# An attention loop in periods of two steps: one whole and two half visits of values, and one pair of score blocks reduced through a relu of key differences

## The chip, the cores and the metric

The kernel runs on one core of a Trainium2 chip. The core has five engines that run beside each other and meet through semaphores: TensorE (PE, with its weight loads shown as PEld), VectorE (DVE), ScalarE (ACT), GpSimd (POOL) and SyncE (SP, which issues the DMAs here). The metric is the device time of one execution in microseconds (us); the text gives the median of several runs.

## What is computed

One transformer block on x of 2048 rows by 448 columns, in float32: a layer norm, attention with 16 query heads of 28 columns that share one key and one value head, a residual add, a second layer norm, a gated feed-forward part of 1792 columns, and a second residual add.

```python
q = (x @ wq).reshape(B, S, H, Dh).transpose(0, 2, 1, 3)     # x here: the normed x
k = x @ wk
v = x @ wv
scores = jnp.einsum("bhqd,bkd->bhqk", q, k) * (Dh ** -0.5)
p = softmax(scores)
o = jnp.einsum("bhqk,bkd->bhqd", p, v)
h = x_in + o.transpose(0, 2, 1, 3).reshape(B, S, H * Dh) @ wo
h2 = h + (silu(n(h) @ w1) * (n(h) @ w3)) @ w2               # n: layer norm
```

## The kernel before

**Numbers.** Most operands are kept as a rounded high part and a low part (fp32r); a product is then three matmuls: high by high, high by low, low by high. For the scores, `KH` and `KL` are the keys' parts, and `QS[i]` holds the queries' (`qh`, `ql`). Values and exponentials are plain float32, whose matmul the chip runs as two passes: each appears twice in the profile.

**Units of work.** Four heads lie in the four strips of 32 rows (`lane(j)`), so four score matmuls with 32 rows each can run side by side. A *unit* i of the attention is one block of 512 queries by four heads; there are 16. A unit has 16 *chunks* of 128 keys, and a *step* s is one chunk of one unit: 256 steps in all.

**What a step does.** For each of the four heads, three matmuls put the transposed scores of 128 keys by 512 queries into a PSUM bank (`Head.mm`, line 293; parts a, b and c of the order below), ACT takes the exponential (`Head.exp`, line 302) into a tile `pt`, and `pv` (line 310) multiplies it with the values `VA[:, c]` into the accumulator `po`. In `pv` the four heads stand side by side in strips of 32 columns, and not of rows. A visit of `pv` takes either all 512 queries of a chunk or a half of them.

**The maxima.** The exponentials need each query's maximum score. It is found 20 steps ahead (`AHEAD`): in each step four *units of the maximum* (class `Unit`, named u0 to u3 after the head) multiply 128 queries by 512 keys (line 241) into a bank, and DVE reduces it (line 246). When a unit i is through, `max_done` (lines 270 to 275) takes the maximum over the four key blocks on DVE, moves it on POOL and transposes it on DVE, and `max_out` (line 281) sends it by four DMAs into a spare row (28 of each strip) of the queries, against which the keys have a row of ones: so the score matmul subtracts the maximum itself. The first 20 steps' maxima are found in the start by `quad` (lines 251 to 268), in another way: since max(a, b) = max(b - a, 0) + a, a matmul with the difference of two key blocks (`KD`) goes through a relu on ACT (line 263), and DVE adds the scores of the first block and takes the maximum in one instruction (line 266), one for two blocks.

**The order of the work** is written out by hand. Every engine takes its instructions in the order in which the code emits them. `ORDER` (line 34) is the order of one step: `3a` is part a of head 3, `u2` the maximum of head 2 (matmul and reduction), `w` and `v` are visits of the values. In each step `w` takes the second half of the chunk of two steps ago, and `v` the first half of the last one (`values`, lines 589 to 598). The last 20 steps have no maxima; they follow `LAST_ORDER`, with whole visits. After the visit `v` and at the end of a step, `run` issues what `todo` holds for this step: splits of the next queries (`build_qs`, line 218), the copy and normalisation of an output (lines 314 to 334), output projections (`wo_rows`, lines 341 to 351, with statistics after it), layer norms and their transposes, and loads of weights.

**Banks and buffers.** Seven PSUM banks go round through a list (`bank`, `done`); the eighth is `po`. In SBUF, `qs_pool` has three buffers of 8 KB per partition for the queries (of which half is used) and later for the feed-forward weights (`split_w`), and `p_pool` four buffers of 4 KB, each for the exponentials of two heads, later for the hidden columns.

**Start and end.** The start (to about 95 us) loads, norms and transposes x, and makes keys, values, queries and the first maxima. After the loop comes the feed-forward part, where PE is busy throughout.

Of the kernel before, what the change touches and what calls it, by code (L numbers as in the profile page):

```python
# [16 lines left out]
P = 128  # L17
S = 2048
D = 448
# [14 lines left out]
ORDER = "3a u2 w 0a 2a u1 3b 1a 0b 2b 3c 1b 0c 2c u3 v u0 1c".split()  # L34
# [4 lines left out]
def block_kernel(  # L39
# [25 lines left out]
    qs_pool = ctx.enter_context(tc.tile_pool(name="qs", bufs=3))  # L65
# [9 lines left out]
    pexp = keep.tile([P, NQ], F32, name="pexp")  # L75
    KH = keep.tile([P, S], F32R, name="KH", tag="kh")
# [139 lines left out]
    def build_qs(i, ps=None):  # L216
        t, g = divmod(i, NG)
        QS[i] = qs_pool.tile([P, 4, T], F32R, name="qs")
        qh, ql = QS[i][:, 0], QS[i][:, 1]
        q = QR[t][:, g] if ps is None else ps  # L220
        se.activation(qh, q, AF.Copy)  # L221
        (ge if ps is None else ve).tensor_tensor(ql, q, f(qh), op=ALU.subtract)  # L222
# [7 lines left out]
    class Unit:  # L230
# [5 lines left out]
        def mm(self):  # L236
            i, n, kt, r = self.i, self.n, self.kt, lane(self.j)
            if i not in MX:
                MX[i] = wk_pool.tile([P, 16, 4], F32, name="mx")
            self.ps = bank("pa")  # L240
            pe.matmul(self.ps, QS[i][r, 0, n * P : (n + 1) * P], KH[r, kt * T : (kt + 1) * T],  # L241
                      start=True, stop=True)

        def red(self):
            c = 4 * self.j + self.n
            ve.tensor_reduce(MX[self.i][:, c, self.kt : self.kt + 1], self.ps, axis=AX.X, op=ALU.max)  # L246
            done(self.ps)
# [3 lines left out]
    def quad(i, n, kp, diff):  # L251
        for j in range(4):
            if i not in MX:
                MX[i] = wk_pool.tile([P, 16, 4], F32, name="mx")
                ge.memset(MX[i], LOW)
            ps = RL[j, diff] = bank("pa")
            ks = KD[:, kp] if diff else KH[:, 2 * kp * T : (2 * kp + 1) * T]
            pe.matmul(ps, QS[i][lane(j), 0, n * P : (n + 1) * P], ks[lane(j)], start=True, stop=True)
        for j in range(4):
            ps = RL.pop((j, diff))  # L260
            if diff:
                r = RL[j] = (wk_pool if j % 2 else sp).tile([P, T], F32, name="rb", bufs=2)
                se.activation(r, ps, AF.Relu)
            else:
                r = RL.pop(j)
                ve.tensor_tensor_reduce(r, ps, r, 1.0, LOW, op0=ALU.add, op1=ALU.max,
                                        accum_out=MX[i][:, 4 * j + n, 2 * kp : 2 * kp + 1])
            done(ps)
# [8 lines left out]
    def max_out(i):  # L277

        dst = f(QS[i][28::32, 0]).rearrange("j (n b x) -> j n b x", n=NQ, b=4)
        for b in range(4):  # L280
            sy.dma_start(dst[:, :, b], NGT[i % 2][32 * b : 32 * b + 16])

    class Head:
# [14 lines left out]
        def exp(self):  # L298
            i, c, (p, jj) = self.i, self.c, divmod(self.j, 2)
            if (i, c, p) not in PT:  # L300
                PT[i, c, p] = p_pool.tile([P, 2, T], F32R, name="pt")
            se.activation(f(PT[i, c, p][:, jj]), self.ps, AF.Exp, bias=0.0, scale=SCALE)  # L302
            done(self.ps)

    def pv(i, c, h0, h1):
# [3 lines left out]
        for j in range(4):  # L309
            pe.matmul(PO[i][32 * j : 32 * j + 32, q], VA[:, c], f(PT[i, c, j // 2][:, j % 2, q]),  # L310
# [71 lines left out]
    with tc.tile_pool(name="start", bufs=1) as sp:  # L382
        wq_r = wo_r = OT[:, :, :D]
        WQ = [w.rearrange("p c (h r) -> p c h r", h=H) for w in OS]
        wkv_r = sp.tile([P, 4, 96], F32, name="wkv_r")
        WKV = [sp.tile([P, 4, 96], F32R, name=f"WKV{k}") for k in range(2)]
        KD = sp.tile([P, 2, T], F32R, name="KD")
        ones = NGT[1][:64]
        ve.memset(wkv_r, 0.0)
        ve.memset(ones, 1.0)  # L390
        ve.memset(VA, 1.0)
        ve.memset(f(NEG[0]), 0.0)
        for k in range(2):
            ve.memset(f(WQ[k][:, :, :, DH:]), 0.0)
        for m0, w in ((0, wk), (64, wv)):
            load_w(wkv_r[:, :, m0 : m0 + DH], w)
        sy.dma_start(X[1], xv[1])
        load_w(wq_r, wq)
        for t in range(2, NT):
            sy.dma_start(X[t], xv[t])  # L400

        def split_wkv():
            ve.tensor_copy(wkv_r[:, :, 32 : 32 + DH], wkv_r[:, :, :DH])
            se.activation(WKV[0], wkv_r, AF.Copy)
            ge.tensor_tensor(WKV[1], wkv_r, f(WKV[0]), op=ALU.subtract)

        wq4 = wq_r.rearrange("p c (h r) -> p c h r", h=H)

        def low_wq(c0, c1, eng):
            for c in range(c0, c1 + 1):  # L410
                eng.tensor_tensor(WQ[1][:, c, :, :DH], wq4[:, c], f(WQ[0][:, c, :, :DH]), op=ALU.subtract)

        def split_wq(c0, c1, eng=None):
            for c in range(c0, c1 + 1):
                se.activation(WQ[0][:, c, :, :DH], wq4[:, c], AF.Copy)
                if eng:
                    low_wq(c, c, eng)

        def load_wo():
            ge.memset(wo_r, 0.0)  # L420
            wov = wo.rearrange("(g j r) e -> j r g e", j=4, r=DH)
            for j in range(4):
                sy.dma_start(wo_r[32 * j : 32 * j + DH], wov[j])

        def split_wo(g):
            ve.tensor_copy(WO[0][:, g], wo_r[:, g])
            ge.tensor_tensor(WO[1][:, g], wo_r[:, g], f(WO[0][:, g]), op=ALU.subtract)

        def stats(t, *ns):
            for n in ns:  # L430
                ln_stats(t, n)
            if NQ - 1 in ns:
                ln_rstd(t)

        def norm(t):
            for n in range(NQ):
                ln_norm(t, n)

        def tr(t, *cs):
            for c in cs or range(4):  # L440
                ln_tr(t, c)

        def kv(t, between=None):
            cols = slice(t * T, (t + 1) * T)
            ps = bank()
            mm_D(ps[:96], WKV, XT[t], slice(0, 96), slice(0, T), between)
            se.activation(KH[0:64, cols], ps[0:64], AF.Copy)
            ve.tensor_tensor(KL[0:64, cols], ps[0:64], f(KH[0:64, cols]), op=ALU.subtract)
            vt = sp.tile([P, T], F32, name="vt", bufs=2)
            se.activation(vt[64:96], ps[64:96], AF.Copy)  # L450
            sy.dma_start(f(KH[64:128, cols]), f(KH[0:64, cols]))
            sy.dma_start(f(KH[28::32, cols]).rearrange("j (b e) -> j b e", b=16), ones)
            sy.dma_start(f(KL[64:128, cols]), f(KL[0:64, cols]))
            if t % 2:
                ge.tensor_tensor(KD[:, t // 2], f(KH[:, cols]), f(KH[:, (t - 1) * T : t * T]), op=ALU.subtract)
            done(ps)
            return vt

        def va(t, vt):
            ps = bank()  # L460
            for n in range(NQ):
                pe.transpose(ps[:, 32 * n : 32 * n + 32], vt[64:96, n * P : (n + 1) * P], ident[64:96, 64:96])
            ve.tensor_copy(VA[:, NQ * t : NQ * t + NQ, :DH],
                           ps[:, :P].rearrange("p (n r) -> p n r", n=NQ)[:, :, :DH])
            done(ps)

        def q(t, g, between=None):
            ps = bank()
            mm_D(ps, [w[:, :, 4 * g : 4 * g + 4].rearrange("p c h r -> p c (h r)") for w in WQ],
                 XT[t], slice(0, P), slice(0, T), between)  # L470
            if t == g == 0:
                build_qs(0, ps)
            else:
                se.activation(QR[t][:, g], ps, AF.Copy)
            done(ps)

        first = [(quad, i, n, 0, diff) for i, n in ((0, 0), (0, 1), (0, 2), (0, 3), (1, 0)) for diff in (True, False)]
        first += [(quad, 0, n, 1, diff) for n in range(NQ) for diff in (True, False)]
        first += [(max_done, 0), (max_out, 0)]
        first += [(quad, 1, 0, 1, diff) for diff in (True, False)]  # L480

        def quads(n=1):
            while n > 0 and first:
                fn, *args = first.pop(0)
                fn(*args)
                n -= fn is quad

        for n in range(NQ):
            ln_stats(0, n)
            ln_rstd(0, n, n + 1)  # L490
            if n > 0:
                ln_norm(0, n - 1)
# [265 lines left out]
```

## Time and profile before

| what | value |
|---|---|
| median of 3 runs | 1238.77 us (1237.6 to 1239.81) |
| the profiled execution | 1238.6 us, span of its instructions 1236.8 us |
| mean granted TensorE clock | 0.998 |
| busy: PE, PEld, DVE, ACT, POOL | 1209.7, 723.4, 869.2, 677.9, 335.6 us |
| visits of the values, instructions of L310 | 3936 matmuls of 400 ns (eight a visit) |
| exponentials, L302 | 1024 of 604 ns |
| maxima, L246 | 944 of 682 ns |
| score matmuls, L293 (KH, KL) | 2048 of 451 ns, 1024 of 420 ns |

A row of the page's groups reads: line, engine, operation, output<-inputs by the names of the code, shape, number of instructions, then busy time in us and the mean duration of one in ns, then the idle time of that engine just before them, and what ended most of it. Matmuls on different strips overlap, so their summed durations are far more than the busy time. In the page's second part the span is cut into 40 slices, and each digit is the busy share in tenths. In a timeline, a row has its start and its length in us; consecutive instructions of one kind are merged into one row (x4), and the bracket tells how long the engine stood idle before it and what ended that. In the windows view a row has the stretch and its length, then for PE, PEld, DVE, ACT and POOL the busy time with the number of instructions, then the granted clock, the DMA share and the GB/s.

### The profile page before, as it was taken

Reading aid. Unit: us, or ns where it says so; the run is one execution under the profiler, and the core shown is the slowest. Engines: PE = TensorE matmul, PEld = TensorE weight load, DVE = VectorE, ACT = ScalarE, POOL = GpSimd, SP = SyncE. Lnnn points to the kernel's source line nnn. Section 1 sums busy time; section 2 is a strip of 40 time slices with the busy share of each in tenths; the row PEclk is TensorE's granted clock in tenths of the full one; section 3 lists DMA queues with packets and bytes.
Section 4 is the critical chain, followed back from the end, with each engine's and each line's share of the span. In section 5 each row is a group of like instructions: output and inputs, shape, how many; then the busy total and the mean of one; then the engine's idle time right before and its main releaser. Section 6 shows DMA issues by size and latency. Waiting matters only on the chain. (4 is left out here: it accounts for less than half of the span.)

```text
span 1236.8 us, 25401 instructions
## 1 busy us (share of the span) xinstructions
PE 1209.7 (98%) x10492; PEld 723.4 (58%) x10492; DVE 869.2 (70%) x1473; ACT 677.9 (55%) x1291; POOL 335.6 (27%) x266
## 2 busy tenths in 40 slices
PE   6999999999999999999999999999999999999998
PEld 4664444444444444444444443488888888888886
DVE  7759999998899998889998893145444445444333
ACT  3657888886688886688786688721111111121111
POOL 3201101110111110121110110454555555555552
PEclk9999999999999999999999999999999999999999
DMA  5010101000010000010000010013000000000000
GB/s 170 10 36 1 34 3 45 11 11 2 11 28 19 11 12 2 11 36 11 11 11 2 10 45 10 26 57 113 1 8 23 2 1 30 1 1 30 1 1 30
DMA packets 32651, 27.03 MB, mean 22 GB/s; under 512 B 11096, under 2 KB 29208, under 8 KB 32536
## 3 DMA queue, kind: packets, MB, share of 16 engines
q1 hardware_dynamic: 32536, 25.41, 7.1%
q8 instruction: 82, 1.34, 0.5%
q14 instruction: 33, 0.27, 0.1%
HBM read 20.25 MB, written 3.80 MB: 19 GB/s over the span
## 5 line engine op out<-in xcount | busy, mean ns | idle before, releaser
L302 ACT ACTIVATE pt<-pb 128x512 f32<-128x512 f32 x1024 | 530.7, 604 | 144.5 <-PE pb L293 121.4
L246 DVE TENSOR_REDUCE mx<-pa 128x1 f32<-128x512 f32 x944 | 585.7, 682 | 16.6 <-PE pa L241 6.9
L293 PE MATMUL pb<-qs,KH 32*128 32x512 f32 x2048 | 368.1, 451 | 3.2 <-ACT pt L302 0.3
L241 PE MATMUL pa<-KH,qs 32*128 32x512 f32 x944 | 346.2, 467 | 4.0 <-DVE mx L246 1.6
L310 PE MATMUL po<-pt,VA 128*32 128x256 f32 (+1 forms) x3936 | 326.8, 400 | 0.5 <-ACT OT L314 0.5
L293 PE MATMUL pb<-qs,KL 32*128 32x512 f32 x1024 | 275.0, 420 | 0.0
L293 PEld LDWEIGHTS pb<-qs,KH 32*128 32x128 f32 x2048 | 166.6, 182 | 140.4 <-ACT pt L302 89.6
L135 PE MATMUL pa<-xh,qs 128*128 128x512 f32 x784 | 205.6, 395 | 0.0
L241 PEld LDWEIGHTS pa<-KH,qs 32*128 32x128 f32 x944 | 140.6, 181 | 101.7 <-DVE mx L246 93.8
L650 ACT ACTIVATE rb<-pa 128x512 f32<-128x512 f32 x56 | 30.4, 596 | 252.6 <-PE pa L642 252.6
L135 PEld LDWEIGHTS pa<-xh,qs 128*128 128x128 f32 x784 | 146.9, 188 | 33.7 <-issue 1.2
L310 PEld LDWEIGHTS po<-pt,VA 128*32 128x32 f32 x3936 | 79.8, 108 | 135.4 <-issue 126.2
L667 PE MATMUL pb<-w2s,pt 128*128 128x448 f32 x672 | 144.5, 370 | 0.8 <-POOL w2s L365 0.8
L667 PEld LDWEIGHTS pb<-w2s,pt 128*128 128x128 f32 x672 | 123.9, 188 | 20.9 <-issue 10.1
L293 PEld LDWEIGHTS pb<-qs,KL 32*128 32x128 f32 x1024 | 116.0, 183 | 0.9
L357 POOL TENSOR_TENSOR qs<-QR,qs 128x1024 fp32r<-128x1024 f32 x32 | 88.1, 2768 | 98.5 <-DVE qs L356 98.5
L659 DVE TENSOR_TENSOR pt<-rb,pt 128x512 fp32r<-128x512 f32 x56 | 82.4, 1471 | 39.2 <-ACT pt L658 39.2
L356 DVE CAST qs<-QR 128x1024 fp32r<-128x1024 f32 x32 | 21.0, 688 | 120.1 <-PE pa L642 96.3
L135 PE MATMUL pa<-xl,qs 128*128 128x512 f32 x336 | 96.3, 395 | 0.0
L658 ACT ACTIVATE pt<-rb 128x512 fp32r<-128x512 f32 x56 | 35.4, 633 | 81.4 <-DVE rb L655 81.4
L222 POOL TENSOR_TENSOR qs<-QR,qs 128x512 fp32r<-128x512 f32 x15 | 19.3, 1285 | 203.2 <-ACT qs L221 187.1
L135 PEld LDWEIGHTS pa<-xl,qs 128*128 128x128 f32 x336 | 63.3, 189 | 14.8
(100 smaller groups left out, 821.1 us busy)
## 6 DMA issues: line engine op xcount, KB each, us to landing
rb<-sd SPq DMA_DIRECT2D x64, 64.0 KB
QR<-in_B_w_dram SPq DMA_DIRECT2D x16, 192.0 KB
X<-in_A_x_dram SPq DMA_DIRECT2D x3, 896.0 KB
out_dram<-X SPq DMA_DIRECT2D x3, 896.0 KB
w<-in_B_w_dram SPq DMA_DIRECT2D x8, 192.0 KB
w_wo<-in_B_w_dram SPq DMA_DIRECT2D x6, 224.0 KB
qs<-ngt SPq DMA_DIRECT2D x64, 2.0 KB
sm<-OT SPq DMA_DIRECT2D x64, 2.0 KB
```

The lines of the kernel that those rows point to most:

```text
L135: pe.matmul(ps, lhs[b][:, cb, lsl], rhs[a][:, ca, rsl], start=(k == 0), stop=(k == len(terms) - 1 and not part),)
L241: pe.matmul(self.ps, QS[i][r, 0, n * P : (n + 1) * P], KH[r, kt * T : (kt + 1) * T], start=True, stop=True)
L246: ve.tensor_reduce(MX[self.i][:, c, self.kt : self.kt + 1], self.ps, axis=AX.X, op=ALU.max)
L293: pe.matmul(self.ps, (KH, KH, KL)[k][r, c * P : (c + 1) * P], QS[i][r, (0, 1, 0)[k]], start=(k == 0), stop=(k == 2))
L302: se.activation(f(PT[i, c, p][:, jj]), self.ps, AF.Exp, bias=0.0, scale=SCALE)
L310: pe.matmul(PO[i][32 * j : 32 * j + 32, q], VA[:, c], f(PT[i, c, j // 2][:, j % 2, q]), start=(c == 0 and h0 == 0), stop=(c == NC - 1 and ...
L356: ve.tensor_copy(wh, W13[k])
L357: ge.tensor_tensor(wl, W13[k], f(wh), op=ALU.subtract)
L650: se.activation(sg, ps[0], AF.Silu)
L658: se.activation(h[:, 0], sg, AF.Copy)
L659: ve.tensor_tensor(h[:, 1], sg, f(h[:, 0]), op=ALU.subtract)
L667: pe.matmul(Y[t][n][:, :D], hid[a][:, n * P : (n + 1) * P], w2s[:, b, :D], start=(k == 0 and m == 0), stop=(k == NF - 1 and m == 2))
```

## The change

1. The loop with maxima goes by *periods of two steps* s and s+1, with one hand-written order for both. Heads 0 to 3 are those of step s, 4 to 7 those of step s+1; `4c'` and `5c'` are the last parts of the previous period's heads.
2. The values of a period take three visits in place of four: `p0` is a whole visit (step s-2), `p1` and `p2` the two halves of step s-1.
3. Of the eight maxima of a period, two become one pair by the difference of keys, as in the start: `d2` is the matmul with `KD` and a relu on ACT, `t2` the matmul with the first of the two key blocks and DVE's add-and-max. The other six stay as they are.
4. `KD` and the relu's buffer stay for the whole loop. The columns of the maxima become two fixed tiles that are set to a very low value once, at the beginning; the column of the second block of a pair keeps it.
5. In SBUF, ten slots of 4 KB per partition take the place of the pools `qs`, `pt` and `start`: three for the queries, five for the exponentials, one each for `KD` and the relu; in the start and in the feed-forward part the same slots hold other tiles. Each exponential takes the next free half of a slot.
6. What `todo` holds for steps s and s+1 is issued at the end of the period; what stands at half steps comes after `p0`. The transposes of the second layer norm move by one step, to whole periods.

```diff
-ORDER = "3a u2 w 0a 2a u1 3b 1a 0b 2b 3c 1b 0c 2c u3 v u0 1c".split()
+ORDER = ("4c' 5c' u3 p0 d2 0a u1 3a 3b 2a 0b 0c u1 2b 3c p1 "
+         "7a u0 1a 2c 1b 6a 7b 1c u0 6b 7c p2 5a 4a u3 6c 4b 5b t2").split()
...
-    qs_pool = ctx.enter_context(tc.tile_pool(name="qs", bufs=3))
...
+    MXS = [keep.tile([P, 16, 4], F32, name=f"mx{k}") for k in range(2)]
+    slots = ctx.enter_context(tc.tile_pool(name="slots", bufs=1))
+
+    def slot(k, dt, name):
+        return slots.tile([P, 2, T], dt, name=name, tag=f"slot{k}")
+
+    QSP, PTP, WSP, HIDP = [4, 0, 1], [9, 5, 6, 7, 8], [(0, 1), (2, 3), (4, 5)], [6, 7, 8, 9]
+    KD = slot(2, F32R, "kd")
+    RELU = slot(3, F32, "relu")
+
+    def take(ring):
+        ring.append(ring.pop(0))
+        return ring[-1]
...
-        QS[i] = qs_pool.tile([P, 4, T], F32R, name="qs")
+        QS[i] = slot(QSP[i % 3], F32R, "qs")
+        MX[i] = MXS[i % 2]
...
-        def mm(self):
+        def mm(self, diff=False):
...
-            pe.matmul(self.ps, QS[i][r, 0, n * P : (n + 1) * P], KH[r, kt * T : (kt + 1) * T],
-                      start=True, stop=True)
+            ks = KD[:, kt // 2] if diff else KH[:, kt * T : (kt + 1) * T]
+            pe.matmul(self.ps, QS[i][r, 0, n * P : (n + 1) * P], ks[r], start=True, stop=True)
...
+        def relu(self, r):
+            se.activation(r, self.ps, AF.Relu)
+            done(self.ps)
+
+        def both(self, r):
+            ve.tensor_tensor_reduce(r, self.ps, r, 1.0, LOW, op0=ALU.add, op1=ALU.max, accum_out=self.col())
+            done(self.ps)
...
-            i, c, (p, jj) = self.i, self.c, divmod(self.j, 2)
-            if (i, c, p) not in PT:
-                PT[i, c, p] = p_pool.tile([P, 2, T], F32R, name="pt")
-            se.activation(f(PT[i, c, p][:, jj]), self.ps, AF.Exp, bias=0.0, scale=SCALE)
+            if not pair:
+                tl = slot(take(PTP), F32, "pt")
+                pair.extend((tl[:, 0], tl[:, 1]))
+            pt = PT[self.i, self.c, self.j] = pair.pop(0)
+            se.activation(pt, self.ps, AF.Exp, bias=0.0, scale=SCALE)
...
-        ws = qs_pool.tile([P, 4, T], F32R, name="qs")
-        wh, wl = [ws[:, 2 * b : 2 * b + 2].rearrange("p a (c m e) -> p (a c) m e", c=2, m=2) for b in range(2)]
+        wh, wl = [slot(x, F32R, "w").rearrange("p a (c m e) -> p (a c) m e", c=2, m=2) for x in take(WSP)]
...
-            at(e + 33.5 + 2 * c, lambda t, c: ln_tr(t, c, True, True), t, c)
+            at(e + 34.5 + 2 * c, lambda t, c: ln_tr(t, c, True, True), t, c)
...
+    for s in range(0, LAST - AHEAD, 2):
+        us = [u for k in range(2) for u in a_units(s + k + AHEAD)]
+        for op in ORDER:
+            x = int(op[1]) if op[0].isalpha() else 0
+            if op[0] == "p":
+                if s > 0:
+                    pv(*divmod(s - 2 + (x > 0), NC), max(x, 1) - 1, x or 2)
+                if x == 0:
+                    run(s + 0.5)
+            elif op[0] == "d":
+                us[x].mm(True)
+                us[x].relu(RELU[:, s // 2 % 2])
+            elif op[0] == "t":
+                us[x].mm()
+                us[x].both(RELU[:, s // 2 % 2])
+            elif op[0] == "u":
+                u = us[x] if us[x] else us[4 + x]
+                us[x] = None
+                u.mm()
+                u.red()
+            else:
+                h = int(op[0])
+                head(s + h // 4 - 2 * (op[-1] == "'"), h % 4, "abc".index(op[1]))
+        run(s)
+        run(s + 1)
...
-            h = p_pool.tile([P, 2, T], F32R, name="pt")
+            h = slot(take(HIDP), F32R, "hid")
```

The rest of the diff indents the start anew and follows from these lines.

More of the change, by code (lines that the diff above doesn't have):

```diff
@@ L251, in quad @@
     def quad(i, n, kp, diff):
[L252 to L268, printed above, removed]
+        us = [Unit(i, n, 2 * kp, j) for j in range(4)]
+        for u in us:
+            u.mm(diff)
+        for u in us:
+            r = (RELU, RELU2)[u.j // 2][:, u.j % 2]
+            u.relu(r) if diff else u.both(r)
     def max_done(i):
@@ L281, in max_out @@
             sy.dma_start(dst[:, :, b], NGT[i % 2][32 * b : 32 * b + 16])
+    pair = []
     class Head:
@@ new lines, in va, with q @@
+    def va(t, vt):
+        ps = bank()
+        for n in range(NQ):
+            pe.transpose(ps[:, 32 * n : 32 * n + 32], vt[64:96, n * P : (n + 1) * P], ident[64:96, 64:96])
+        ve.tensor_copy(VA[:, NQ * t : NQ * t + NQ, :DH],
+                       ps[:, :P].rearrange("p (n r) -> p n r", n=NQ)[:, :, :DH])
+        done(ps)
+    def q(t, g, between=None):
+        ps = bank()
+        mm_D(ps, [w[:, :, 4 * g : 4 * g + 4].rearrange("p c h r -> p c (h r)") for w in WQ],
+             XT[t], slice(0, P), slice(0, T), between)
+        if t == g == 0:
+            build_qs(0, ps)
+        else:
+            se.activation(QR[t][:, g], ps, AF.Copy)
+        done(ps)
@@ new lines, in block_kernel, with quads @@
+    first = [(quad, i, n, 0, diff) for i, n in ((0, 0), (0, 1), (0, 2), (0, 3), (1, 0)) for diff in (True, False)]
+    first += [(quad, 0, n, 1, diff) for n in range(NQ) for diff in (True, False)]
+    first += [(max_done, 0), (max_out, 0)]
+    first += [(quad, 1, 0, 1, diff) for diff in (True, False)]
+    def quads(n=1):
+        while n > 0 and first:
+            fn, *args = first.pop(0)
+            fn(*args)
+            n -= fn is quad
+    for n in range(NQ):
+        ln_stats(0, n)
+        ln_rstd(0, n, n + 1)
+        if n > 0:
+            ln_norm(0, n - 1)
@@ new lines, in block_kernel @@
+    ln_norm(0, NQ - 1)
+    split_wkv()
+    tr(0, 0, 1)
+    stats(1, 0)
+    tr(0, 2)
+    stats(1, 1)
+    tr(0, 3)
+    split_wq(0, 1, ge)
+    split_wq(2, 3)
+    stats(1, 2, 3)
+    v0 = kv(0)
+    norm(1)
+    tr(1)
+    low_wq(2, 3, ve)
+    v1 = kv(1)
+    stats(2, 0, 1, 2, 3)
+    q(0, 0)
+    q(0, 1)
+    norm(2)
+    va(0, v0)
+    va(1, v1)
+    quads()
+    q(0, 2, quads)
+    build_qs(1)
+    quads()
+    q(0, 3, quads)
+    tr(2)
+    stats(3, 0, 1, 2, 3)
+    quads()
+    v2 = kv(2)
@@ L547, in block_kernel @@
+    q(1, 0, quads)
+    norm(3)
+    q(1, 1, quads)
+    va(2, v2)
+    quads()
+    q(1, 2, quads)
+    build_qs(2)
+    q(1, 3, quads)
+    tr(3)
+    v3 = kv(3)
+    load_wo()
+    q(2, 0)
+    va(3, v3)
+    q(2, 1)
+    for t, g in ((2, 2), (2, 3), (3, 0), (3, 1)):
+        quads()
+        q(t, g, quads)
+    quads()
+    q(3, 2, quads)
+    q(3, 3)
+    quads(64)
     todo = {}
@@ L583, in run @@
     def run(s):
[L584 removed]
+        for fn, args in todo.pop(s, []):
             fn(*args)
[L587 to L598 removed]
```

267 lines of the change are left out of this document (89 added, 178 removed).

## The prediction

> **What bounds the kernel now.** I read the page's slices first, then one stretch of the windows view, then the timeline of one step, engine by engine.
>
> ```profile
> PE   6999999999999999999999999999999999999998
> DVE  7759999998899998889998893145444445444333
> ACT  3657888886688886688786688721111111121111
> ```
> ```profile
> 200.00:300.00 100.00, 99.63 (x1232) 44.81 (x1228) 95.65 (x161) 80.53 (x157) 9.52 (x11) 1.00 0.03 8
> ```
> ```profile
> L246 DVE TENSOR_REDUCE mx<-pa x944: 627/681/695, 94.5 to 750.9; 128x1 f32<-128x512 f32 x189
> ```
>
> The profiled execution takes 1238.6 us with a span of 1236.8, against a median of 1238.77: the sum below starts from 1238.6. The change touches the 236 attention steps that hold the 944 reductions (four a step, so 118 pairs of steps), from 94 to 751 us: 656 us, 5.56 a pair. The start and the feed-forward part do the same work as before. In the loop PE and DVE both look full (99.6 and 95.7 of 100 us), and busy shares can't say which of them paces it. The weight loads of one ordinary step can.
>
> ```profile
> 420.97 0.16 PEld L310 LDWEIGHTS po<-pt,VA 128*32 128x32 f32 x8 [0.27 <-issue]
> 421.54 0.18 PEld L241 LDWEIGHTS pa<-KH,qs 32*128 32x128 f32 x1 [0.41 <-DVE mx L246]
> ...
> 421.99 0.16 PEld L310 LDWEIGHTS po<-pt,VA 128*32 128x32 f32 x8 [0.24 <-issue]
> 422.56 0.18 PEld L293 LDWEIGHTS pb<-qs,KH 32*128 32x128 f32 x2 [0.41 <-ACT pt L302]
> ...
> 422.93 0.18 PEld L293 LDWEIGHTS pb<-qs,KH 32*128 32x128 f32 x1
> ...
> 423.49 0.16 PEld L310 LDWEIGHTS po<-pt,VA 128*32 128x32 f32 x8 [0.28 <-issue]
> ```
> ```profile
> 422.91 0.42 PE L293 MATMUL pb<-qs,KL 32*128 32x512 f32 x1
> 423.15 0.39 PE L293 MATMUL pb<-qs,KH 32*128 32x512 f32 x1
> ```
>
> The step is 423.49 - 420.97 = 2.52 us, and PE fills it with four pieces: a half visit of the values (L310) of 0.57 (to 421.54), a group of four score matmuls of 0.45 (to 421.99), a half visit of 0.57 (to 422.56), a group of twelve of 0.93. Inside the twelve the four row strips work in rounds of four: starts at 422.56, 422.91, 423.15. One round costs 0.45 and three cost 0.93, so a further round costs 0.24, and 0.21 of each group is the change between the strips of the scores and the columns of the values. The waits named in brackets lie behind the visit that is running.
>
> ```profile
> 420.92 2.06 ACT L302 ACTIVATE pt<-pb 128x512 f32<-128x512 f32 x4 [0.46 <-PE pb L293]
> 423.44 2.07 ACT L302 ACTIVATE pt<-pb 128x512 f32<-128x512 f32 x4 [0.45 <-PE pb L293]
> ```
> ```profile
> 248.96 2.06 ACT L302 ACTIVATE pt<-pb 128x512 f32<-128x512 f32 x4 [0.45 <-PE pb L293]
> 252.12 2.06 ACT L302 ACTIVATE pt<-pb 128x512 f32<-128x512 f32 x4 [1.10 <-PE pb L293]
> 254.63 2.07 ACT L302 ACTIVATE pt<-pb 128x512 f32<-128x512 f32 x4 [0.44 <-PE pb L293]
> ```
> ```profile
> 300.79 4.25 DVE L246 TENSOR_REDUCE mx<-pa 128x1 f32<-128x512 f32 x7
> ```
>
> Seven reductions end to end take 4.25 us at 0.68 each, so one starts (4.25 - 0.68) / 6 = 0.60 after the other, and a step's four take 2.40. Four exponentials take 2.06 at 0.60 each: 0.49 apart, 1.95 a step. So PE paces the ordinary step, DVE is 0.12 behind it, ACT has 0.56 to spare.
>
> **The change, part by part.** *The visits.* Per pair of steps, four half visits become one whole and two halves. The last twenty steps of before have whole visits:
>
> ```profile
> 759.71 0.22 PEld L310 LDWEIGHTS po<-pt,VA 128*32 128x32 f32 x8 [0.37 <-issue]
> 760.77 0.30 PEld L293 LDWEIGHTS pb<-qs,KH 32*128 32x128 f32 x8 [0.84 <-issue]
> 761.11 0.19 PEld L293 LDWEIGHTS pb<-qs,KL 32*128 32x128 f32 x4
> 761.67 0.15 PEld L310 LDWEIGHTS po<-pt,VA 128*32 128x32 f32 x6 [0.37 <-issue]
> ```
>
> A whole visit is 1.06, of which 0.06 is a wait (its eight loads take 0.22, not 0.16): 1.00. Twelve matmuls with nothing late take 0.90 here.
>
> *The order.* The 32 score matmuls of a pair stood in groups of 4, 12, 4, 12: eight full rounds. They now stand in groups of 11, 11 and 10. Taking the strips in the written order (2 0 1 3, 3 2 0, 0 1 2 3 for the first group), each needs three rounds: nine in all, one of them made up of holes. So one change of shape (0.21) and 0.14 of visit are saved, and a round of 0.24 is given back. PE's new period: 1.00 + 2 x 0.57 + 3 x (0.90 to 0.93) = 4.84 to 4.93; I take 0.92 for a group, as the loop runs now: 4.90, against 5.03 by ACT's starts (423.44 - 420.92 = 2.52, 254.63 - 252.12 = 2.51). That is 0.13 x 118 = 15.3 us less, with ends of 22.4 less (4.84) and 4.7 less (4.99, with 1.06 for the whole visit).
>
> *The relu pair.* Of eight reductions six remain (3.60); two become a matmul on the key difference, a relu on ACT and an add-and-max on DVE. The start of before has the same pair:
>
> ```profile
> L263 ACT ACTIVATE rb<-pa x40: 592/606/678, 32.1 to 89.3; 128x512 f32<-128x512 f32 x40
> ```
> ```profile
> 35.83 0.69 DVE L266 CUSTOM_DVE_ANT_0 rb<-pa,rb 128x512 f32<-128x512 f32 x1
> 36.44 0.08 DVE L266 DVE_READ_ACCUMULATOR2_ANT mx<- 128x1 f32 x1
> ```
>
> The add-and-max is 0.61 from start to start, so DVE needs 4.21 of 4.90 (was 4.80 of 5.03). The relu is as long as an exponential, so ACT needs 9 x 0.49 = 4.41 of 4.90 (was 3.92 of 5.03). PE's count of matmuls stays. The relief on DVE thus moves nothing by itself in an ordinary step.
> The Trainium skill speaks against this edit: "ScalarE: Activation LUTs", Rules for kernel authors, wants relu on VectorE, not on ScalarE. Here the trace differs, 0.49 apart on ACT against 0.60 on DVE from the same banks; with the relu on DVE too, DVE would stand at 4.81 of 4.90.
>
> *Does the order wait?* I walk it at the row times, from the whole visit at 0: rounds at 1.00, 1.34, 1.57; half visit 1.92; rounds at 2.49, 2.83, 3.06; half visit 3.41; rounds at 3.98, 4.32, 4.55; end 4.90. An exponential starts 0.53 after its last matmul (422.91 to 423.44). Three banks come back barely in time: 0c (1.57) is read from 2.10 to 2.70, and 6a takes its bank at 2.83; 1c (3.06) from 3.59 to 4.19, t2 at 4.32; t2's add-and-max (after u3's reduction, 4.51) from 5.11 to 5.80, 3a at 5.90. No wait, but no slack either. The max of a unit is now closed at a pair's end and sent one pair later, ahead of its first use by one whole period instead of three steps (SP sends as soon as the transposed max is there): I cost that at nothing, hidden by that period's matmuls; without that cover it would be a wait like the 1.29 of a small DMA quoted below, 15 times, 19 us. POOL's two memsets of the max columns move to the start, among loads that it doesn't hold up.
>
> *What stops a period now and then.* Once per unit of sixteen steps ACT copies the attention output and splits the next queries:
>
> ```profile
> 136.91 2.07 ACT L302 ACTIVATE pt<-pb 128x512 f32<-128x512 f32 x4 [0.44 <-PE pb L293]
> 138.84 0.63 ACT L314 ACTIVATE OT<-po 128x512 f32<-128x512 f32 x1
> 139.43 2.06 ACT L302 ACTIVATE pt<-pb 128x512 f32<-128x512 f32 x4
> 141.35 0.65 ACT L221 ACTIVATE qs<-QR 128x512 fp32r<-128x512 f32 x1
> 141.98 2.07 ACT L302 ACTIVATE pt<-pb 128x512 f32<-128x512 f32 x4
> ```
>
> These take 0.59 and 0.63 of ACT, and now the steps hardly feel it (2.52, 2.55): each lies in its own step with 0.56 spare. In the new loop both fall into one period with 0.49 spare, 0.73 over; with the next whole visit waiting for the copy and 2a and u1 for the late exponentials I reach 0.99. I take 0.8, 13 times: 10.4 more (ends 5 and 14, the lower if neighbours take half of it). The eight layer-norm activations are a lesser case:
>
> ```profile
> 338.78 0.78 ACT L178 ACTIVATE xn<-X,nb,rs 128x448 f32<-128x448 f32 x1
> 339.43 2.08 ACT L302 ACTIVATE pt<-pb 128x512 f32<-128x512 f32 x4
> ```
>
> 0.65 each against 0.49 spare, 0.3 taken (ends 0 and 0.65): 2.4 more.
>
> DVE's own interruptions get a little cheaper:
>
> ```profile
> 308.44 0.62 DVE L163 BATCH_NORM_STATS2 st<-X 128x6 f32<-128x448 f32 x1
> ...
> 309.19 2.45 DVE L246 TENSOR_REDUCE mx<-pa 128x1 f32<-128x512 f32 x4
> ```
> ```profile
> 591.05 0.25 DVE L326 RECIPROCAL sm<-sm 128x16 f32<-128x16 f32 x1 [1.29 <-DMA sm<-OT]
> ```
>
> Closing a unit's max makes a step of 3.16 (248.96 to 252.12, among ACT's rows above), 0.65 over, 15 times; the statistics (0.75) follow each of twelve output projections. DVE's spare time is spread over the period, and the reductions behind the interruption (u1, whose bank 1a needs) are still late, so I keep 0.5 of each 0.65: 15 x 0.15 + 12 x 0.15 = 4.1 less, with ends of 0 and 17.6 less. The reciprocal, queued ahead of the reductions, waited 1.29 for its DMA, twice; it now stands about a microsecond further behind its copy: 1.5 less (ends 0 and 2.6).
>
> *The slots.* The same tiles in other places; the exponentials get five buffers of two heads instead of four. ACT's gaps above end on PE, not on a free buffer, so this is worth nothing, with ends of 1 us either way at the start and end of the loop.
>
> Sum: -15.3 + 10.4 + 2.4 - 4.1 - 1.5 = -8.1, so 1230.5 us.
>
> **The rivals.** *DVE did pace the loop, in its latencies.* For: 95.65 of 100 us, and loads marked as released by it. Against: PE's four pieces add up to the step. Then the period comes to PE's floor of 4.84 (-22.4), half of DVE's interruptions vanish (-8.8), the reciprocal too (-2.6), and ACT's extras are at their lower end (+5): 1210.
> *The ninth round eats the merged visit.* With 1.06 and 0.93 the period is 4.99: -4.7 + 10.4 + 2.4 - 5.6 = +2.5, 1241; in between, no change.
> *ACT becomes the bound (slower).* At 0c, 1c and the relu an activation that starts 0.1 late hands its delay to PE through a bank, and nine must pass in order. Two such waits a period make it 5.10: 0.07 x 118 = 8.3 more, and 8.3 + 10.4 + 2.4 - 5.6 = +15.5: 1254. It decides from a period of about 4.97 on, where 118 periods no longer pay for ACT's extras. For it: the three margins above, all under 0.13. Against: 0.49 of ACT's period is free.
> *Neighbours in one strip expose a weight load (slower).* The first group has 3a 3b and 0b 0c side by side, which nothing in before has. If the second's load (0.18) can't run under the first, the period grows by 0.36: +42, 1273. Against: the third round's loads begin at 422.93 while the second round, started 422.91 in the same strips, is running. This is what the Trainium skill states in "TensorE: Matmul & The Clock Gate", Part 3: a load overlaps a running matmul only in another row group; the trace does not bear it out.
>
> **How the numbers follow.** Forecast 0.50, DVE rival 0.14, ninth round 0.16, ACT 0.15, weight loads 0.05. About 0.2% (2.5 us) is what a measurement of this kernel can tell from no change: 1236.3 to 1241.2. Faster: 0.47 of the forecast, 0.14, 0.01 of the ninth round: 0.62. Same: 0.03 + 0.11 = 0.14. Slower: 0.04 + 0.15 + 0.05 = 0.24. The range takes in the DVE rival and reaches into the ACT one: 1207 to 1250; the forecast's own is 1222 to 1238.
>
> **What would show it.** Right: whole visits of 1.0 and three groups of 0.9, starts 4.90 apart in ordinary periods; 708 reductions and 118 add-and-max in the loop (L246's old rate of 0.60); stretched periods where OT and qs are written. Wrong: a period near 4.84 with short max steps (DVE), loads after the first group's start that wait for ACT (ACT), or gaps of 0.18 between 3a and 3b.

## The result and the profile after

The changed kernel takes 1221.45 us (median of 4 runs, 1221.11 to 1221.75) against 1238.49 before: 17.0 us less, a ratio of 0.9861 with a 95% interval of 0.9844 to 0.9879. The profiled execution takes 1221.11, its span is 1219.2. The forecast was 1230.5: the direction and the range (1207 to 1250) held, the gain of 8.1 was half of the measured one.

The slices of the page after, in the order in which those of before stand above:

```profile
PE   6999999999999999999999999999999999999998
DVE  7758889888888887878887891154444445444333
ACT  3658999997799997899997899610111111121111
```

The windows view of the same 100 us as before, and the reductions of the loop:

```profile
200.00:300.00 100.00, 99.30 (x1085) 46.69 (x1082) 87.52 (x166) 90.89 (x176) 9.50 (x11) 1.00 0.03 7
```
```profile
L261 DVE TENSOR_REDUCE mx<-pa x708: 626/686/694, 94.2 to 734.0; 128x1 f32<-128x512 f32 x177
```

DVE fell from 95.7 to 87.5 of 100 us and ACT rose from 80.5 to 90.9; PE stands at 99 as it did. The loop ends about 17 us earlier (734 for 751), and what comes after it is the same work. One ordinary period, in PE's weight loads:

```profile
409.81 0.18 PEld L255 LDWEIGHTS pa<-kd,qs 32*128 32x128 f32 x1 [0.84 <-ACT pt L317]
...
409.87 0.29 PEld L307 LDWEIGHTS pb<-qs,KH 32*128 32x128 f32 x4
...
410.76 0.16 PEld L325 LDWEIGHTS po<-pt,VA 128*32 128x32 f32 x8 [0.36 <-issue]
411.33 0.18 PEld L307 LDWEIGHTS pb<-qs,KH 32*128 32x128 f32 x1 [0.41 <-DVE mx L261]
...
412.24 0.16 PEld L325 LDWEIGHTS po<-pt,VA 128*32 128x32 f32 x8 [0.29 <-issue]
412.81 0.18 PEld L307 LDWEIGHTS pb<-qs,KH 32*128 32x128 f32 x2 [0.41 <-ACT pt L317]
...
413.71 0.16 PEld L325 LDWEIGHTS po<-pt,VA 128*32 128x32 f32 x8 [0.28 <-issue]
414.70 0.18 PEld L255 LDWEIGHTS pa<-kd,qs 32*128 32x128 f32 x1 [0.84 <-ACT pt L317]
```

The pieces are a group of eleven (409.81 to 410.76, 0.95), a half visit (0.57), eleven (0.91), a half visit (0.57), ten (0.90) and a whole visit (413.71 to 414.70, 0.99): 4.89. The ten matmuls take as long as the twelve of before (0.90 where nothing is late): three rounds each, full or not. So the ordinary period is as forecast (4.90). DVE's timeline shows how even it is, and where it isn't:

```profile
414.01 0.68 DVE L269 CUSTOM_DVE_ANT_0 relu<-pa,relu 128x512 f32<-128x512 f32 x1
...
423.81 0.68 DVE L269 CUSTOM_DVE_ANT_0 relu<-pa,relu 128x512 f32<-128x512 f32 x1
...
425.05 0.21 DVE L287 STREAM_TRANSPOSE ngt<-neg 128x32 f32<-128x32 f32 x1 [0.29 <-POOL neg L286]
...
429.30 0.68 DVE L269 CUSTOM_DVE_ANT_0 relu<-pa,relu 128x512 f32<-128x512 f32 x1
```

Two ordinary periods take 9.80 from add-and-max to add-and-max (414.01 to 423.81), but the one in which a unit's maxima are closed takes 5.49 (423.81 to 429.30); in it DVE's transpose waits 0.29 for POOL's copy.

For a sum over the whole loop I took the start of every eighth exponential as the beginning of a period, in each trace, and compared the 118 periods kind by kind. From its first to its 118th period the loop went from 658.0 to 641.6 us:

| kind of period | before | after |
|---|---|---|
| ordinary | 5.03 | 4.88 |
| closes a unit's maxima | 5.67 | 5.48 |
| copies an output and splits queries; the next one | 5.07, 5.04 | 5.57, 5.07 |
| of these the next one, where a small DMA comes late in before (two cases) | 6.45 | 5.07 to 5.09 |
| four projections with statistics, and the two periods behind them, over as many ordinary ones | 13.7 | 11.5 |

In the last row the 0.60 of a closing, which falls into the first of these periods after, is taken off.

### The profile page after: what moved, and what is told of

It is laid out like the page before. It is cut to its first block, busy times and chain, and to the rows that moved or that the text cites. A ratio compares the mean times of both kernels' runs of the same rounds, so it can differ in the third digit from the quotient of the medians.

```text
span 1219.2 us, 24016 instructions
## 1 busy us (share of the span) xinstructions
PE 1193.9 (98%) x9540; PEld 726.4 (60%) x9540; DVE 802.9 (66%) x1473; ACT 738.8 (61%) x1409; POOL 327.9 (27%) x266
## 4 chain that ended last, share of the span: by engine, by line
PE 91%; ACT 3%; DVE 3%; issue 2%; POOL 1%; DMA 0%; DVEq 0%; ACTq 0%; POOLq 0%
PE po L325 22%; PE pa L149 21%; PE pb L307 20%; PE pb L699 11%; PE pa L255 8%; PE pa L362 3%; PE pb L149 2%; ACT pt L317 2%; PE pa L674 2%; PE pb L208 1%; DVE relu L269 1%; ACT OT L329 1%; DVE st L177 0%; DVE xn L194 0%; DVE mx L261 0%
## 5 line engine op out<-in xcount | busy, mean ns | idle before, releaser
L261 DVE TENSOR_REDUCE mx<-pa 128x1 f32<-128x512 f32 x708 | 462.5, 685 | 68.6 <-PE pb L307 55.3
L149 PE MATMUL pa<-xh,w 128*128 128x512 f32 x784 | 205.6, 395 | 0.0
L149 PEld LDWEIGHTS pa<-xh,w 128*128 128x128 f32 x784 | 146.9, 188 | 33.7 <-issue 1.2
L699 PE MATMUL pb<-w2s,hid 128*128 128x448 f32 x672 | 144.5, 370 | 0.8 <-POOL w2s L379 0.8
L699 PEld LDWEIGHTS pb<-w2s,hid 128*128 128x128 f32 x672 | 123.9, 188 | 20.9 <-issue 10.1
L265 ACT ACTIVATE relu<-pa 128x512 f32<-128x512 f32 x158 | 92.0, 607 | 51.9 <-PE pa L255 49.3
L269 DVE CUSTOM_DVE_ANT_0 relu<-pa,relu 128x512 f32<-128x512 f32 x158 | 105.6, 683 | 16.9 <-PE pa L255 16.9
L371 POOL TENSOR_TENSOR w<-QR,w 128x1024 fp32r<-128x1024 f32 x32 | 83.9, 2636 | 100.3 <-PE pa L674 85.3
L691 DVE TENSOR_TENSOR hid<-rb,hid 128x512 fp32r<-128x512 f32 x56 | 71.9, 1284 | 39.2 <-ACT hid L690 39.2
L149 PE MATMUL pa<-xl,w 128*128 128x512 f32 x336 | 96.3, 395 | 0.0
L255 PEld LDWEIGHTS pa<-kd,qs 32*128 32x128 f32 x158 | 24.2, 181 | 90.9 <-ACT pt L317 72.1
```

What stands on the lines that cost most here:

```text
L149: pe.matmul(ps, lhs[b][:, cb, lsl], rhs[a][:, ca, rsl], start=(k == 0), stop=(k == len(terms) - 1 and not part),)
L255: pe.matmul(self.ps, QS[i][r, 0, n * P : (n + 1) * P], ks[r], start=True, stop=True)
L261: ve.tensor_reduce(self.col(), self.ps, axis=AX.X, op=ALU.max)
L265: se.activation(r, self.ps, AF.Relu)
L269: ve.tensor_tensor_reduce(r, self.ps, r, 1.0, LOW, op0=ALU.add, op1=ALU.max, accum_out=self.col())
L371: ge.tensor_tensor(wl, W13[k], f(wh), op=ALU.subtract)
```

## The experiments

Ten kernels, in three groups that each ran on one chip; in each group before was 1237.9 to 1238.5 us. The first four take the change apart: its frame, its relu pair and its visits.

**e0_frame: the new loop and slots, the old order.** ORDER is that of two old steps (with `w0 v0 w1 v1` for the four half visits) and holds eight plain reductions.

```diff
-ORDER = ("4c' 5c' u3 p0 d2 0a u1 3a ... 4b 5b t2").split()
+ORDER = ("3a u2 w0 0a 2a u1 3b 1a 0b 2b 3c 1b 0c 2c u3 v0 u0 1c "
+         "7a u2 w1 4a 6a u1 7b 5a 4b 6b 7c 5b 4c 6c u3 v1 u0 5c").split()
```

> The changed kernel's loop and slots, but the old order (four half visits a period, groups of 4, 12, 4, 12) and eight plain reductions. PE theory (visits and rounds of matmuls set the ordinary period): 5.03 a period as before; what is left of the change, the slots and the issuing at the period's end, gives -3 to 0: 1235 to 1239 us. Rival, that the slots or the other issue times gave a good part of the 17 us: under 1232 us.

1229.98 us, ratio 0.9924 (0.9905 to 0.9944): half of the whole gain, without a new order and without the pair. That is the rival's side. Ordinary periods are 5.03 and those that close the maxima 5.67, as before. What changed are the projections (12.0 over, where before has 13.7) and the two late DMAs, which are gone. DVE around two projections of this kernel:

```profile
298.72 0.62 DVE L364 TENSOR_TENSOR X<-pa,X 128x448 f32<-128x448 f32 x1 [2.24 <-PE pa L361]
...
302.37 0.62 DVE L176 BATCH_NORM_STATS2 st<-X 128x6 f32<-128x448 f32 x1
...
306.60 0.62 DVE L364 TENSOR_TENSOR X<-pa,X 128x448 f32<-128x448 f32 x1 [1.63 <-PE pa L361]
```

In before the statistics stood right behind their own projection's add (307.30, then 308.44), when banks were already waiting for DVE. Issued at the period's end, they stand 3.6 us behind the add, and the delay that they make runs into the next projection, during which DVE waits for PE anyway: its idle time falls from 2.24 to 1.63 and nothing is late. Only the last of four has no projection behind it and costs its 0.64.

**e1_pair: the same with the relu pair.**

```diff
-ORDER = ("3a u2 w0 ... 7a u2 w1 ...
+ORDER = ("3a d2 w0 ... 7a t2 w1 ...
```

> As the last one, with the relu pair (head 2) in the old order: the relief of DVE alone. PE theory: the ordinary period stays at 5.03, and only DVE's interruptions (maxima closed, statistics) get cheaper: 1228 to 1236 us. DVE theory (the reductions paced the loop): ordinary period 4.85, 1212 to 1220 us.

1224.8 us, ratio 0.9884 (0.9868 to 0.9900), 5.2 less than e0. The starts of ACT's runs of exponentials, period by period:

```profile
240.08 2.07 ACT L316 ACTIVATE pt<-pb 128x512 f32<-128x512 f32 x4 [0.44 <-PE pb L306]
...
245.10 2.06 ACT L316 ACTIVATE pt<-pb 128x512 f32<-128x512 f32 x4 [0.45 <-PE pb L306]
...
250.18 2.07 ACT L316 ACTIVATE pt<-pb 128x512 f32<-128x512 f32 x4 [0.49 <-PE pb L306]
```

The ordinary period is 5.02 (240.08 to 245.10), not 4.85: in the old order PE paces it, and the DVE theory is out. But the period that closes the maxima (245.10 to 250.18) takes 5.08, where e0 has 5.67: DVE now has a reduction's time to spare in each period, and in this order it can use it. Added up over the loop, some 7 us come from there, 3 from the projections and 1 from the loop's first periods, and some 6 go back in ACT's periods (5.45 in place of 5.07 with the output's copy and the queries, 5.57 in place of 5.09 with a layer norm).

**e2_plain: the new order with eight plain reductions.**

```diff
-... p0 d2 0a u1 ... 4b 5b t2
+... p0 u2 0a u1 ... 4b 5b u2
```

> The new order with the merged visit, but two plain reductions in the places of d2 and t2: the visits alone. PE theory as it was forecast (the pair moves nothing by itself in an ordinary period): 4.9 to 4.95, 1225 to 1233 us. Bank theory (the order holds only because the relu takes a reduction out of DVE's queue; without it 1a and u0 wait for banks that DVE holds, some 0.4 to 0.5 a period): 5.3 to 5.4, 1270 to 1285 us. DVE theory: DVE at 4.81 of reductions, near 5.0, 1235 to 1245 us.

1268.38 us, ratio 1.0236 (1.0209 to 1.0263). This order needs the pair: the period is the one of the bank theory (5.3 to 5.4), the time just under its range. PE's weight loads of one period:

```profile
212.59 0.18 PEld L306 LDWEIGHTS pb<-qs,KH 32*128 32x128 f32 x1 [0.41 <-DVE mx L260]
212.59 0.18 PEld L254 LDWEIGHTS pa<-KH,qs 32*128 32x128 f32 x1
212.95 0.18 PEld L306 LDWEIGHTS pb<-qs,KH 32*128 32x128 f32 x1 [0.18 <-DVE mx L260]
...
213.98 0.16 PEld L324 LDWEIGHTS po<-pt,VA 128*32 128x32 f32 x8 [0.24 <-issue]
```

The second group begins with two loads (212.59), and the third, 1a, comes 0.36 later, released by DVE: its bank was u1's, and u1's reduction now stands behind u2's. The group takes 1.39 (212.59 to 213.98) in place of 0.91, the period 5.37 in place of 4.88.

**e3_plain_best: eight reductions with the merged visit, in another order.** The order was arranged anew for the fewest late banks: `5a' u3 5b' 6c' 4b' 5c' u3 4c' u2 p0 2a u0 3a 1a 2b 1b 3b u0 2c 1c 3c 0a u2 p1 0b 7a 0c 7b 6a u1 6b 7c u1 p2 4a`.

> Eight plain reductions with one whole and two half visits, in an order arranged anew so that by a walk at the rows' durations the fewest banks come late. PE theory: 4.9, 1225 to 1233 us. Bank theory: no order of eight reductions runs at PE's floor, since DVE's 4.81 leaves no room for the idle stretches around the visits: 5.05 to 5.15, 1238 to 1252 us, no better than before.

1241.31 us, ratio 1.0021 (1.0011 to 1.0032), with ordinary periods of 5.08. DVE's sixteen reductions in a row:

```profile
199.67 10.23 DVE L260 TENSOR_REDUCE mx<-pa 128x1 f32<-128x512 f32 x16
```

One every 0.64, eight in 5.09. But end to end eight take 4.80, so DVE has 0.29 to spare, and PE's weight loads show another cause:

```profile
200.97 0.18 PEld L306 LDWEIGHTS pb<-qs,KH 32*128 32x128 f32 x1 [0.84 <-DVE mx L260]
...
202.08 0.16 PEld L324 LDWEIGHTS po<-pt,VA 128*32 128x32 f32 x8 [0.30 <-issue]
...
206.05 0.18 PEld L306 LDWEIGHTS pb<-qs,KH 32*128 32x128 f32 x1 [0.84 <-DVE mx L260]
```

The first group takes 1.11 (200.97 to 202.08). It holds thirteen matmuls, four of them in one strip (2a, 2b, 2c and u2), and so needs four rounds: this order has ten rounds where the changed kernel has nine. With groups of 0.93 and 0.90, two half visits and a whole one, PE's own pieces come to 5.08. So e3 hits the number of the bank theory (5.05 to 5.15) by luck and does not test it: whether eight reductions can run with the merged visit in nine rounds, at 4.9, stays open.

The second group tests what stretches single periods.

**e9_before_later: the kernel before, with two entries of its plan one step later.**

```diff
-        at(e + 2, o_norm, i % NG)
+        at(e + 3, o_norm, i % NG)
...
-            at(e + 14 + 2 * n, ln_stats, t, n)
+            at(e + 15 + 2 * n, ln_stats, t, n)
```

> The kernel before with two entries of its plan one step later: the statistics after an output projection (so that they stand right before the next projection, during which DVE is idle) and the reciprocal of the sums (so that DVE doesn't wait for the small DMA). If these two are what the changed loop's frame gained: 5 for the statistics and 2.8 for the two waits of 1.3 to 1.4: 1230 to 1232 us. Rival (the slots, or fewer waits for the exponentials' buffers, gave it): 1236 us or more.

1230.82 us, ratio 0.9941 (0.9923 to 0.9959). Two numbers in the old kernel give 7.6 us, nearly all that the frame gives (8.5). The reciprocal that had waited 1.29 us at 591.05 in before no longer does, and the statistics stand where e0 has them. Both parts are in its trace: the projections are at 12.0 over, as in e0, and the two periods of 6.45 are at 5.03.

```profile
587.66 0.24 DVE L326 RECIPROCAL sm<-sm 128x16 f32<-128x16 f32 x1
```

**e4_qs_pool: the changed kernel with the queries' copy on POOL.**

```diff
-        se.activation(qh, q, AF.Copy)
+        if ps is None and i > 2:
+            ge.tensor_copy(qh, q)
+        else:
+            se.activation(qh, q, AF.Copy)
```

> The changed kernel, but the copy of the next queries' high part (line 236) runs on POOL in place of ACT. ACT theory (the copy of the output and the split of the queries fall into one period and cost 0.87 together there): that period goes from 5.57 + 5.07 to about 5.35 + 4.9, 0.4 less in some ten units: 1216.5 to 1219 us. Rival (the output's copy alone costs it, by holding the accumulator): no change, 1221 us.

1217.54 us, ratio 0.9830 (0.9812 to 0.9847), 3.9 under the changed kernel. First ACT in the changed kernel, then in this one:

```profile
394.81 0.60 ACT L265 ACTIVATE relu<-pa 128x512 f32<-128x512 f32 x1 [0.17 <-PE pa L255]
...
397.93 0.62 ACT L329 ACTIVATE OT<-po 128x512 f32<-128x512 f32 x1
...
398.88 0.66 ACT L236 ACTIVATE qs<-QR 128x512 fp32r<-128x512 f32 x1
...
400.36 0.66 ACT L265 ACTIVATE relu<-pa 128x512 f32<-128x512 f32 x1
```
```profile
393.15 0.60 ACT L268 ACTIVATE relu<-pa 128x512 f32<-128x512 f32 x1 [0.18 <-PE pa L258]
...
398.45 0.60 ACT L268 ACTIVATE relu<-pa 128x512 f32<-128x512 f32 x1
```

From relu to relu the period with both copies takes 5.55 (394.81 to 400.36), and ACT has no gap in it; with the output's copy alone it takes 5.30 (393.15 to 398.45). The period behind it falls from 5.07 to 4.84.

**e7_turn: the transpose of a unit's maxima half a period later.** `max_done` keeps the reduction and POOL's copy; DVE's transpose is issued after the next `p0`, behind another reduction.

```diff
         ge.tensor_copy(neg[:, :16], nm)
-        ve.transpose(NGT[i % 2], f(neg))
+
+    def max_turn(i):
+        ve.transpose(NGT[i % 2], f(NEG[i % 2]))
...
+        at(NC * i - 3.5, max_turn, i)
         at(NC * i - 4, max_out, i)
```

> The changed kernel, but when a unit's maxima are closed, DVE's transpose is issued half a period later than its reduction, so that DVE doesn't stand 0.3 waiting for POOL's copy in between. Theory that DVE's delay goes on to PE through u1's bank one for one, as the walk has it: the period of 5.48 becomes 5.15 to 5.2, 15 times 0.3: 1216 to 1218 us. Rival (the delay is set by the reduction itself and the bank chain behind it): 1220 to 1222 us.

1216.29 us, ratio 0.9822 (0.9806 to 0.9837), 5.2 less than the changed kernel, 0.34 on average for each of 15. DVE in that period:

```profile
421.60 0.68 DVE L269 CUSTOM_DVE_ANT_0 relu<-pa,relu 128x512 f32<-128x512 f32 x1
...
422.46 0.68 DVE L261 TENSOR_REDUCE mx<-pa 128x1 f32<-128x512 f32 x1
423.06 0.20 DVE L289 STREAM_TRANSPOSE ngt<-neg 128x32 f32<-128x32 f32 x1
...
426.69 0.68 DVE L269 CUSTOM_DVE_ANT_0 relu<-pa,relu 128x512 f32<-128x512 f32 x1
```

A reduction now fills the time in which POOL copies, and the period takes 5.09 (421.60 to 426.69) in place of 5.49.

**e8_all: both, and the layer norms of the loop on POOL.**

```diff
-            se.activation(xn[:, :D], X[t][:, n], AF.Identity, bias=nb[:, n : n + 1], scale=rs[:, n : n + 1])
+            ge.tensor_scalar(xn[:, :D], X[t][:, n], mv[:, n, 0:1], rs[:, n : n + 1],
+                             op0=ALU.subtract, op1=ALU.mult)
```

> Both of these, and the eight layer-norm activations on POOL in place of ACT: what keeps the ordinary period from showing in the sum is taken off ACT and DVE. If the interruptions are what ate the 17 us of the merged visit: the gains add up, 4 and 4.5 and 2 to 3: 1209 to 1213 us. If PE has other waits behind them: 1215 us or more.

1208.37 us, ratio 0.9757 (0.9742 to 0.9773): 13.1 less than the changed kernel and 30 less than before, the best version of the study. The first two gains (3.9 and 5.2) leave 4 for the third: the layer norms' periods go from 5.2 to 5.4 down to 4.9, but for those behind a closing (5.45 to 5.05). The ordinary period stays at 4.88.

The third group asked what remains.

**e10_halves_all: e8 with the old visits.** The edits of e8 upon e1_pair.

> The last version with everything taken off ACT and DVE, but with the old visits (four halves, groups of 4, 12, 4, 12) and the relu pair in the old order: what the merged visit is worth when the interruptions are small. If its 0.145 a period comes through once they are gone, this kernel is 14 to 17 us over the 1208.4 of the merged one: 1222 to 1225 us, hardly under the pair alone (1224.8). If the old order gains from the relief as well (output copy and queries 0.42 a unit, layer norms 0.5 each): 1214 to 1218 us, and the merged visit is worth 6 to 10 even then.

1216.99 us, ratio 0.9826 (0.9811 to 0.9840). With the interruptions relieved, the merged visit is worth 8.6 us (1216.99 to 1208.37, on two chips on which before differs by 0.5); without that it was worth 3.4 (e1 to the changed kernel). Its 0.145 a period would be 17 us over 118 periods. The remainder goes to the tighter period still: the close of the maxima costs 0.2 there (5.05 to 5.11 where 4.88 is ordinary) and 0.05 in the old order (5.07 where 5.03 is), the output's copy 0.43 (5.31) against 0.04 (5.07).

**e11_tr_dve: e8, with the low part of the transposes taken by DVE from the bank.**

```diff
-            at(e + 34.5 + 2 * c, lambda t, c: ln_tr(t, c, True, True), t, c)
+            at(e + 34.5 + 2 * c, lambda t, c: ln_tr(t, c, False, True), t, c)
```

> The same best version, but in the eight transposes of the second layer norm the low part is taken by DVE straight from the bank, without ACT's second copy. If ACT's 0.48 a transpose is what makes those periods 5.93 to 6.68: 0.3 to 0.45 less in each of eight: 1205 to 1206.5 us. If PE's transposes and their change of shape make it, or DVE is then late instead: 1208 to 1210 us.

1210.6 us, ratio 0.9775 (0.9759 to 0.9792), 2 more than e8 and over both expectations. Most periods with a transpose got 0.2 longer (5.94 to 6.14), and the one behind the last rose to 5.53 (4.84 and 5.12 in e8); only the one with the output's copy got shorter, from 6.38 to 5.91. In DVE's queue the subtraction now stands ahead of u1's reduction and waits for ACT:

```profile
350.94 0.69 DVE L223 TENSOR_TENSOR xl<-pb,xh 128x512 fp32r<-128x512 f32 x1 [1.14 <-ACT xh L216]
351.55 2.55 DVE L265 TENSOR_REDUCE mx<-pa 128x1 f32<-128x512 f32 x4
```

So ACT's second copy is gone, but a wait for DVE stands in its place. What makes the 5.94 is better seen in e8's own trace:

```profile
354.70 0.42 PEld L209 LDWEIGHTS pb<-ident,xn 128*128 128x128 f32 x4 [0.84 <-ACT pt L323]
355.29 0.18 PEld L259 LDWEIGHTS pa<-kd,qs 32*128 32x128 f32 x1 [0.17 <-issue]
...
356.76 0.18 PEld L313 LDWEIGHTS pb<-qs,KH 32*128 32x128 f32 x1 [0.41 <-ACT rb L220]
...
357.52 0.19 PEld L313 LDWEIGHTS pb<-qs,KH 32*128 32x128 f32 x2 [0.20 <-ACT pt L323]
...
358.18 0.16 PEld L331 LDWEIGHTS po<-pt,VA 128*32 128x32 f32 x8 [0.36 <-issue]
```

PE's four transposes take 0.59 before the group can start (354.70 to 355.29), and the second group takes 1.42 (356.76 to 358.18) in place of 0.91, with a wait for ACT inside it. The two add up to 0.59 + 0.51 = 1.10, about the whole excess over 4.88 (1.06); a kernel that changes PE's part was not run.

## Why the prediction was right or wrong

**What bounds the loop: right.** The four pieces of PE, the rounds, the price of a whole visit (1.00 forecast, 0.99 measured) and of a group with holes (0.92; 0.95, 0.91, 0.90) gave a period of 4.90; it is 4.88. The tenth round of e3, at 0.2, fits the same count. The forecast's -15.3 us for ordinary periods is -17 (0.145 x 118). e1 is the test against the DVE rival: the relief alone leaves the old order at 5.03.

**"The relief on DVE thus moves nothing by itself in an ordinary step": right for the old order, wrong for the new one.** e0 and e1 are both at 5.03; but the new order without the pair is at 5.37 (e2). I costed visits and pair as two edits, each by the engine that it loads. In this order they are one: with a reduction more in DVE's queue its banks come late. The walk over the banks had the means to see it: with u2's reduction ahead of u1's, 1a's bank comes 0.36 late. I walked only the order as it stood. That no other order of eight reductions could do it is not shown, since e3's has a round more.
The rule of the Trainium skill against relu on ScalarE ("ScalarE: Activation LUTs", Rules for kernel authors) would put the relu on DVE. By DVE's count that is eight such instructions again, 4.8 of a period of 4.88, and with eight reductions this order takes 5.37 (e2). A relu on DVE itself was not run, so no run here tests that rule.

**The ninth round, the weight loads: as forecast.** The page "TensorE: Matmul & The Clock Gate" (Part 3) of the Trainium skill would have had two exposed loads of 0.18 in the first group, where 3a 3b and 0b 0c stand side by side; that group takes 0.95 against 0.91 and 0.90 for the others. The trace has another cause for the 0.05: 3a loads at 409.87, 0.06 behind the group's first, because its bank is that of t2, whose add-and-max on DVE ends at 409.81. So nothing of the 0.36 shows; but of the three banks that the walk had "barely in time", this one is late.

**ACT's copies and the layer norms: right in kind and nearly in size.** Output and queries together were put at 0.8 and take 0.87 over two ordinary periods (5.57 - 4.88 and 5.07 - 4.88), where before had 0.05; over the loop that is about 9 us for the 10.4 forecast. e4 shows the mechanism. The layer norms came to 2.2 (forecast 2.4).

**"I keep 0.5 of each 0.65": the step that failed.** I lumped two interruptions of DVE together and gave both a small discount. Closing the maxima hardly got cheaper (0.60 over where 0.64 stood: 0.6 us in all, where 2.25 was forecast), since the reductions behind it are late by DVE's wait for POOL as well; e7, which fills that wait of 0.29, takes 0.40 off the period. The statistics, on the other hand, cost nothing any more for three in four, since the new place of their issue puts their delay into the next projection's shadow. Point 6 of the change has them issued at the period's end; I costed only the length of the instruction there, not what follows it on PE. Projections and statistics gave 3 x 2.2 = 6.6 us, where 1.8 was forecast for the statistics: no other term of the sum was so far off. e0 and e9 show that most of it needs neither the new order nor the pair: 5.1 of the 6.6 are there in e9's trace, that is in the old kernel.

**The reciprocal: right in kind, half in size.** Both waits vanished whole (2.8 for 1.5).

**The slots: worth nothing, as forecast,** as far as e0 and e9 tell: 1229.98 and 1230.82, in two groups of runs. Outside the loop the profile is some 1 us shorter; its cause was not looked for.

**The sum.** Forecast were gains of 20.9 (15.3, 4.1 and 1.5) and losses of 12.8 (10.4 and 2.4). The two traces show gains of about 28 (ordinary periods 17, projections and maxima 7, the reciprocal 3, outside the loop 1) and losses of about 11 (copies 9, layer norms 2), and the profiled times differ by 17.5. DVE's interruptions were off by 3 us as a whole (7 for 4.1, with the statistics 5 too small and the maxima 1.7 too large), every other term by less than 2; but all erred to the same side, and in a difference of two large sums that made a factor of two. As to the range, the upper end (1250) was set by an ACT rival that the trace contradicts: ACT was busy 90.9 of 100 us, and of the three banks with narrow margins one came late in ordinary periods, by 0.06, and not by 0.1 twice.

## What to carry to other kernels

When an engine is full, write its period as pieces with durations from the trace (visits, rounds, changes of shape), and then walk the other engines' queues through that period, also with each part of the change left out: a part that seems to move nothing can be what the rest depends on. Count the rounds of an order that is meant as a comparison, too: e3 differs from the changed kernel by a round, and not by its reductions alone. A tighter ordinary period has less room for what comes now and then, so price those interruptions in the new period, and move what can be moved to an idle engine (here POOL) or behind another instruction. Look at what stands behind an instruction that is moved: here a delay right before a long stretch of another engine cost nothing, and such a place was found by changing one number in a plan.

## What the runs showed of the hardware

A group of ten matmuls in four row strips took as long (0.90 us) as one of twelve. The strips advanced in rounds: in the group of ten the matmuls start at 412.81, 413.14 and 413.37, and a strip left empty in a round saved nothing. A fourth round, for one matmul, made a group 1.11 (e3). POOL's copy of 128x512 to fp32r took 0.62 us and hardly disturbed DVE and ACT: in e4 the reductions beside it took 0.69 us, as in the same place of other ordinary periods, and the exponentials 0.62 to 0.64 against 0.61 to 0.63.
